# Table scatters moved ahead of the squares in the router's steps of an attention and mixture-of-experts kernel

## The chip, the cores and the metric

One core of a Trainium2 chip runs the whole program. The core has a matrix engine (TensorE, PE in the rows, with its weight loads as PEld), a vector engine (VectorE, DVE), an activation engine (ScalarE, ACT), a general engine (GpSimd, POOL) and an engine whose queue only issues DMAs here (SyncE, SP). Each works through its own queue in order and waits there for semaphores. The metric is the device time of one execution in microseconds (us), the median of the runs.

## What is computed

Block-causal attention over 8 batches, 8 heads, 576 places and a head size of 64, whose output rows are then routed, each to one of 8 experts:

```python
scores = np.where(block_i >= block_j, scale * q @ k.T, -1e9)     # blocks of 64
attn = softmax(scores);  x = (attn @ v) rearranged to (4608, 512)
xn = x / (norm(x) + 1e-6);  en = emb / (norm(emb) + 1e-6)
logits = xn @ en.T / tau
expert_idx = argmax(logits);  gate_w = softmax(logits)[expert_idx]
for e in range(8):
    h = relu(x[expert_idx == e] @ w1[e])
    out[expert_idx == e] = gate_w * (h @ w2[e])
```

## The kernel before

The attention takes the first 460 us or so, the experts the rest. The attention runs over 32 pairs of heads, four pairs for a batch. An iteration of its loop works on several pairs at once, each in another stage, and the order of the stages' steps is written out by hand: a string of letters (`PLANS`), one for each of the four places in a batch and four more for the last batch, in which each letter runs one step of a generator. Since each engine's queue is in order, these strings set the order of the work on all engines.

The letters: `s`, scores of the pair: PE's two matmuls (lines 368 and 369) into one of two PSUM buffers (`pss`), ACT's exp out of it (378, 385), POOL's adds of the exps over the key tiles (359), which later give the softmax sums. `v`, values of the pair before: matmuls of the exps with v (400), then the matmuls with ones over POOL's sums (409, 410, 414) and copies out by DVE (416) and ACT (418). `m`, row maxes of the next pair: PE's matmuls (337) into one of two buffers (`psm`), DVE's reductions out of them (339), at the end a transpose whose cast on ACT (346) is written into the queries' operand by SP (348). `p`, preparation two pairs ahead: transposes (296), casts on ACT (308, 312, 317), subtractions on DVE (287), copies by SP (310, 320). `f`, the finish of the pair before: transposes and matmuls (436 to 441) and DVE's scaling (446 to 459). `l`, loads. `r`, one step of the router, if one is at work.

The router of a batch (`route`, line 483) is appended when the batch's last pair is finished, which is in the first iteration of the next batch, and then gives one step to every `r`. It sums the heads' logits, takes the arg max as a one-hot `ohb`, counts the tokens ahead of each by small matmuls, and then, for all batches but the last:

- five `squares` (line 478): the sums of squares of the batch's 512-wide rows, on ACT, one for each tile of 128 tokens;
- the square root of them, a power on POOL (554);
- `table_rows` (634 to 644): six small DVE operations that give each token its place in a table in DRAM;
- the gate: add (558), reciprocal (560), product with the logits (562) on DVE, exp on ACT (564), sum, add and reciprocal on DVE (566 to 570), the last into the batch's rows `xrow`;
- `store` (473, 474): two DMAs on SP's queue that write the batch's rows with their gates, 1040 KB, to DRAM;
- five scatters (576): indirect DMAs that POOL issues, each writing 128 token numbers to the table at the places that `table_rows` gave. They don't read the squares, the gate or the rows.

Each of these operations ends its step, but the store is one step. Counted by the letters, in a usual batch the squares come at the end of the second iteration and the start of the third, power and table rows at places 11 to 23 of the third, the gate from place 39 of the third to place 3 of the fourth (in which values' sums, lines 409 to 414, stand at place 33), the store at place 5 and the scatters at places 6 to 12. After the scatters the router is done and the remaining letters `r` are empty. In the last-but-one batch, whose plans differ, a further generator (`early_rows`, 601 to 607) reads a part of the table back and gathers two tiles of rows.

Of the kernel before, what the change touches and what calls it, by code (L numbers as in the profile page):

```python
# [34 lines left out]
def kernel(  # L35
# [12 lines left out]
    nc = tc.nc  # L48
    B, H, S, D = q.shape
    E, DM, DF = w1.shape  # L50
    NT = B * S
    P = 128
    NP = H // 2
    NJ = (S - 64) // P + 1
# [16 lines left out]
    RE = (NT + P - 1) // P  # L71
# [3 lines left out]
    table = dram.tile([E * RE * P, 1], F32, name="table")  # L75
# [19 lines left out]
    def iota(name, shape, pattern, base=0, cm=0, dt=F32):  # L95
        t = const.tile(shape, dt, name=name)
        nc.gpsimd.iota(t, pattern=pattern, base=base, channel_multiplier=cm, allow_small_or_imprecise_dtypes=True)
        return t
# [3 lines left out]
    tokf = iota("tokf", [P, B, NJ], [[S, B], [P, NJ]], 1 - 64, 1)  # L102
# [377 lines left out]
    def bc(ap, *shape):  # L480
        return ap.to_broadcast(shape)

    def route(b, xrow, lgh, ssp):

        lg = sm.tile([P, NJ, E], F32, name="lg")
# [2 lines left out]
        ohb = sm.tile([P, NJ, E], BF16, name="ohb")  # L488
# [29 lines left out]
        if b < B - 1:  # L518
            t2 = above(rk, ebase)
# [11 lines left out]
        if b == B - 2:  # L531
# [11 lines left out]
            nc.vector.tensor_copy(accb, acc)  # L543
            yield

        ss = sm.tile([P, NJ], F32, name="ss")
        gs = sm.tile([P, NJ], F32, name="gs")
        if b < B - 1:
# [4 lines left out]
            nc.vector.tensor_reduce(ss, ssp, axis=AX.X, op=ALU.add)  # L553
        nc.gpsimd.tensor_tensor(ss, ss, half, op=ALU.pow)
        yield
        if b < B - 1:
            rowj = yield from table_rows(t2, ohb)
        nc.vector.tensor_scalar(ss, ss, 1.0e-6, None, op0=ALU.add)
        yield
        nc.vector.reciprocal(ss, ss)  # L560
        yield
        nc.vector.tensor_tensor(lg, lg, bc(ss.unsqueeze(2), P, NJ, E), op=ALU.mult)
        yield
        nc.scalar.activation(lg, lg, AF.Exp)
        yield
        nc.vector.tensor_reduce(gs, lg, axis=AX.X, op=ALU.add)
        yield
        nc.vector.tensor_scalar(gs, gs, 1.0e-9, None, op0=ALU.add)
# [3 lines left out]
        store(b, xrow, 0 if b < B - 1 else (NP - 1) * P, RW)  # L572
        yield
        if b < B - 1:
            for j in range(NJ):
                w = nc.gpsimd.indirect_dma_start(
                    out=table, out_offset=bass.IndirectOffsetOnAxis(ap=rowj[:, j:j + 1], axis=0),
                    in_=tokf[:, b, j:j + 1], in_offset=None, bounds_check=E * RE * P - 1, oob_is_err=False)
                for o in writes:
                    tc.declare_no_dep(w.ins, o.ins, reason="each place is written once")  # L580
                writes.append(w)
                yield
            if b == B - 2:
                slow.append(early_rows())

    writes, ends = [], []
# [25 lines left out]
    def above(rk, base):  # L612
        t = sm.tile([P, NJ, E], F32, name="t2")
        nc.vector.tensor_tensor(t, rk, base, op=ALU.add)
        return t
# [13 lines left out]
    def table_rows(t, ohb):  # L629

        row = sm.tile([P, NJ], F32, name="row")
        rowt = sm.tile([P, NJ], I32, name="rowt")
        rowj = sm.tile([P, NJ], I32, name="rowj")
        nc.vector.tensor_tensor(t, t, ohb, op=ALU.mult)
        yield
        nc.vector.tensor_reduce(rowj, t, axis=AX.X, op=ALU.max)
        yield
        nc.vector.tensor_scalar(rowt, rowj, P - 1, None, op0=ALU.bitwise_and)
        yield
        nc.vector.tensor_scalar(row, rowt, float(E * RE) - 1.0 / P, None, op0=ALU.mult)  # L640
        yield
        nc.vector.scalar_tensor_tensor(row, rowj, 1.0 / P, row, op0=ALU.mult, op1=ALU.add)
        yield
        nc.vector.tensor_tensor(rowj, row, drop, op=ALU.add)
        yield
        return rowj
# [460 lines left out]
    a, b = ea  # L1107
# [138 lines left out]
```

## Time and profile before

| | us |
|---|---|
| median of 3 runs | 943.08 (940.4 to 945.08) |
| profiled execution | 946.42 |
| its span, first to last instruction | 944.7 |
| PE busy | 903.0 (96%) |
| DVE, ACT, POOL busy | 536.0, 455.8, 335.5 |
| mean granted clock of PE | 0.976 |

The profiled execution has 1.7 us outside its span. Busy times count instructions at work; the granted clock is the share of full speed that the chip gave PE in a stretch. A timeline row gives an instruction's start, its duration, its engine and line, output and input tiles, and in brackets how long the engine had been idle and what released it.

### The profile page before, as it was taken

The numbers are of one execution on the slowest core, as the hardware profiler recorded it, in microseconds if no ns is written. First come the engines' busy times: TensorE is split into PE (matmuls) and PEld (weight loads), VectorE is DVE, ScalarE is ACT, GpSimd is POOL, SyncE is SP. The second block draws the span as 40 slices with busy tenths as digits, with TensorE's granted clock in tenths as the row PEclk, the third lists the DMA queues.
The fourth block names the chain that finished last, engine by engine and source line by source line (L and its number), as shares of the span: only waits on it lengthen the run. The fifth ranks groups of instructions, "written<-read, shape, count | busy, mean of one in ns | idle before, by whom it ended". The sixth has DMA issues, their size and how long they took to land. (4 is left out here: it accounts for less than half of the span.)

```text
span 944.7 us, 19846 instructions
## 1 busy us (share of the span) xinstructions
PE 903.0 (96%) x5429; PEld 706.8 (75%) x5429; DVE 536.0 (57%) x1291; ACT 455.8 (48%) x923; POOL 335.5 (36%) x436
## 2 busy tenths in 40 slices
PE   5999999898999989898999999999999999999996
PEld 4677677677766767665678888888888888888885
DVE  8678778686877858676676634664342222442221
ACT  4566658475565847566655424553432222432220
POOL 6444645556464555546631111111011111111111
PEclk8899989999999999899999999999999999999999
DMA  8958757676886758593737444654242111111101
GB/s 151 179 115 176 177 114 154 150 150 141 166 188 114 156 141 166 132 196 121 244 119 253 135 136 135 216 177 171 78 167 67 46 47 47 47 43 47 46 30 44
DMA packets 155248, 122.47 MB, mean 130 GB/s; under 512 B 122234, under 2 KB 123530, under 8 KB 155101
## 3 DMA queue, kind: packets, MB, share of 16 engines
q1 hardware_dynamic: 147372, 100.14, 44.0%
q0 software_dynamic: 7728, 20.70, 6.8%
q8 instruction: 52, 0.85, 0.4%
q14 instruction: 96, 0.78, 0.3%
HBM read 72.98 MB, written 19.71 MB: 98 GB/s over the span
## 5 line engine op out<-in xcount | busy, mean ns | idle before, releaser
L378 ACT ACTIVATE pT<-pss 128x448 f32<-128x448 f32 (+1 forms) x254 | 112.5, 452 | 111.9 <-PE pss L369 80.4
L339 DVE TENSOR_REDUCE nmx<-psm 128x1 f32<-128x320 f32 x315 | 135.1, 453 | 49.3 <-PE psm L337 38.7
L981 POOL DMA_INDIRECT out_dram<-y,outi x36 | 36.1, 1002 | 356.8 <-DVE y L980 336.6
L368 PE MATMUL pss<-qb,ka 128*128 128x448 f32 (+1 forms) x382 | 128.1, 346 | 17.9 <-ACT pT L378 17.0
L359 POOL TENSOR_TENSOR pS<-pT 128x448 f32<-128x448 f32 x64 | 73.1, 1142 | 155.3 <-ACT pT L378 155.0
L359 POOL TENSOR_TENSOR pS<-pS,pT 128x320 f32<-128x320 f32 (+2 forms) x192 | 114.2, 595 | 29.2 <-ACT pT L378 8.1
L941 PE MATMUL py<-ring_h,hh 128*128 (+1 forms) x288 | 116.4, 404 | 0.4 <-ACT hh L974 0.4
L941 PE MATMUL py<-ring_h,hl 128*128 (+1 forms) x288 | 113.6, 395 | 2.1 <-DVE hl L975 2.1
L941 PE MATMUL py<-ring_l,hh 128*128 (+1 forms) x288 | 112.7, 391 | 0.0
L369 PE MATMUL pss<-qx,kx 70*128 70x448 f32 (+1 forms) x382 | 110.4, 313 | 2.3 <-DMA qx<-nmT 2.3
L400 PE MATMUL psb<-pT,vo 128*64 128x64 f32 (+5 forms) x768 | 111.3, 405 | 1.2 <-DVE lgh L459 1.2
L941 PE MATMUL ph<-ring_h,xh 128*128 x280 | 112.2, 401 | 0.0
L941 PE MATMUL ph<-ring_h,xl 128*128 x280 | 109.7, 392 | 0.0
L941 PE MATMUL ph<-ring_l,xh 128*128 x280 | 109.3, 390 | 0.0
L933 DVE TENSOR_TENSOR xl<-px,xh 128x512 fp32r<-128x512 f32 x35 | 24.2, 690 | 145.4 <-ACTq L908 119.0
L368 PEld LDWEIGHTS pss<-qb,ka 128*128 128x128 f32 x382 | 74.6, 195 | 39.3 <-ACT pT L378 21.2
L974 ACT CAST hh<-px 128x512 fp32r<-128x512 f32 x72 | 38.7, 589 | 134.8 <-PE px L972 134.8
L959 ACT ACTIVATE h<-ph 128x512 f32<-128x512 f32 x70 | 41.8, 597 | 126.1 <-ACTq L908 58.5
L337 PE MATMUL psm<-kd,qd 128*128 128x320 f32 x315 | 91.7, 354 | 3.0 <-ACT kd L317 1.7
L761 DVE TENSOR_TENSOR ring_l<-raw,ring_h 128x1024 f32 (+1 forms) x64 | 77.3, 1248 | 25.3 <-ACT ring_h L757 25.1
L337 PEld LDWEIGHTS psm<-kd,qd 128*128 128x128 f32 x315 | 56.3, 196 | 40.4 <-ACT pT L385 14.6
L980 DVE TENSOR_SCALAR y<-py,xg 128x512 f32<-128x512 f32 x36 | 27.0, 750 | 98.9 <-PE py L941 93.4
(246 smaller groups left out, 1665.3 us busy)
## 6 DMA issues: line engine op xcount, KB each, us to landing
raw<-in_moe_w_dram SPq DMA_DIRECT2D x64, 512.0 KB
ka<-kd SPq DMA_DIRECT2D x128, 144.0 KB
qn<-in_q_dram SPq DMA_DIRECT2D x64, 144.0 KB
kn<-in_k_dram SPq DMA_DIRECT2D x64, 144.0 KB
qx<-qb SPq DMA_DIRECT2D x32, 288.0 KB
vo<-in_v_dram SPq DMA_DIRECT2D x64, 128.0 KB
xbuf<-xrow SPq DMA_DIRECT2D x7, 1040.0 KB
qx<-nmT SPq DMA_DIRECT2D x64, 2.2 KB
```

The costliest lines, as they stand in the source:

```text
L337: nc.tensor.matmul(mx[:, 0:max(e - a, 256)], qd[d][:, j, :, :], kd[d][:, a:a + max(e - a, 256)], start=True, stop=True)
L339: nc.vector.tensor_reduce(m[:, j + u:j + u + 1], mx[:, 0:e - a], axis=AX.X, op=ALU.max, negate=True)
L359: nc.gpsimd.tensor_tensor(o, pT[0:r, P:S] if t == 1 else o, pT[0:r, off[t]:off[t] + w], op=ALU.add)
L368: nc.tensor.matmul(o, ka[i][:, hh, ts], qb[i][:, hh, c0:c1], start=True, stop=False)
L369: nc.tensor.matmul(o, kx[i][0:KX, hh, ts], qx[i][0:KX, hh, c0:c1], start=False, stop=True)
L378: nc.scalar.activation(pT[:, o:o + c1 - c0], st[:, 0:c1 - c0], AF.Exp, scale=scale)
L400: nc.tensor.matmul(ob[hh * D:(hh + 1) * D, c0:c1], a[0:r, t, hh, :], pTs[hh][0][0:r, o:o + c1 - c0], start=(t == 0), stop=(c0 == 448 or t ...
L761: return eng.tensor_tensor(piece(ring_l, to, c, half), raw[i][:, c * CW:(c + 1) * CW], piece(ring_h, to, c, half).bitcast(F32), op=ALU.sub ...
L941: m = nc.tensor.matmul(out, a[:, c, :], w, start=(c == 0 and w is wh and a is sh), stop=(c == nk - 1 and a is sl_))
L959: nc.scalar.activation(h[:, f:f + 512], ph, AF.Relu)
L974: nc.scalar.copy(hh[:, f:f + 4, :], ptv)
L981: nc.gpsimd.indirect_dma_start(out=out, out_offset=bass.IndirectOffsetOnAxis(ap=to, axis=0), in_=y, in_offset=None, bounds_check=NT - 1, o ...
```

## The change

In `route`, for all batches but the last, `table_rows` and the five scatters stand ahead of the squares; the power follows the squares as before; then come seven empty steps, and the gate, with two empty steps ahead of its exp and five behind it. The store is the last step. No operation is added or taken away, and the plans are as before; the router takes 53 letters where it took 39.

```diff
+    def pause(n):
+        for _ in range(n):
+            yield
+
     def route(b, xrow, lgh, ssp):
...
+        if b < B - 1:
+            rowj = yield from table_rows(t2, ohb)
+            for j in range(NJ):
+                w = nc.gpsimd.indirect_dma_start(
+                    out=table, out_offset=bass.IndirectOffsetOnAxis(ap=rowj[:, j:j + 1], axis=0),
+                    in_=tokf[:, b, j:j + 1], in_offset=None, bounds_check=E * RE * P - 1, oob_is_err=False)
+                for o in writes:
+                    tc.declare_no_dep(w.ins, o.ins, reason="each place is written once")
+                writes.append(w)
+                yield
+
         ss = sm.tile([P, NJ], F32, name="ss")
         gs = sm.tile([P, NJ], F32, name="gs")
...
         nc.gpsimd.tensor_tensor(ss, ss, half, op=ALU.pow)
         yield
+
         if b < B - 1:
-            rowj = yield from table_rows(t2, ohb)
+            yield from pause(7)
         nc.vector.tensor_scalar(ss, ss, 1.0e-6, None, op0=ALU.add)
...
+        if b < B - 1:
+            yield from pause(2)
         nc.scalar.activation(lg, lg, AF.Exp)
         yield
+        if b < B - 1:
+            yield from pause(5)
         nc.vector.tensor_reduce(gs, lg, axis=AX.X, op=ALU.add)
...
         store(b, xrow, 0 if b < B - 1 else (NP - 1) * P, RW)
         yield
         if b < B - 1:
-            for j in range(NJ):
-                w = nc.gpsimd.indirect_dma_start(
...
-                yield
             if b == B - 2:
                 slow.append(early_rows())
```

By the letters, in a usual batch the table rows now come at the end of the second iteration and up to place 11 of the third, the scatters at places 13 to 21 of the third (values' sums stand at place 26), the squares at 23, 39, 40, 42 and 55, the power at 56; in the fourth iteration the gate's three first steps at places 12 to 16, its exp at 19, the rest at 34 to 37 and the store at 38, behind values' sums at 33. In the last-but-one batch, the squares come from the end of the second iteration on, the store at place 66 of the third, and the gathers in the fourth.

## Rows read from the trace of the kernel before

The stretch from 93.4 to 123.3 us holds the third and fourth iterations of batch 1, in which the router of batch 0 runs; the other batches repeat it every 55 us.

**Rows 1.** the page, section 1: busy us, share of the span, instructions.

```profile
PE 903.0 (96%) x5429; PEld 706.8 (75%) x5429; DVE 536.0 (57%) x1291; ACT 455.8 (48%) x923; POOL 335.5 (36%) x436
```

**Rows 2.** windows (stretch: length, each engine's busy us, granted clock, DMA share, GB/s).

```profile
55.00:67.70 12.70, 12.70 (x98) 9.22 (x98) 9.53 (x26) 7.70 (x17) 6.38 (x10) 1.00 0.42 90
105.50:123.30 17.80, 14.97 (x97) 11.12 (x97) 10.57 (x33) 8.18 (x18) 11.40 (x15) 0.86 0.45 124
...
sum 103.40, PE 87.66 PEld 64.74 DVE 63.46 ACT 48.47 POOL 67.67; mean PE 14.61 PEld 10.79 DVE 10.58 ACT 8.08 POOL 11.28
```

**Rows 3.** waits of PE, 50 to 480 us: total us, times, longest.

```profile
PE pss L368 <- ACT pT L378: 17.0, 7, 2.8
```

**Rows 4.** timeline, batch 0 (start us, us, engine, line; idle before and its releaser).

```profile
110.56 1.12 POOL L576 DMA_INDIRECT table<-tokf,rowj  x1 [0.58 <-DVE gs L566]
...
113.93 0.46 PE L410 MATMUL psb<-pS,ones 128*32 128x320 f32 x1
114.60 0.42 PE L368 MATMUL pss<-qb,ka 128*128 128x320 f32 x1
115.84 0.97 POOL L576 DMA_INDIRECT table<-tokf,rowj  x1 [0.30 <-issue]
116.82 1.15 POOL L359 TENSOR_TENSOR pS<-pT 128x448 f32<-128x448 f32 x1
118.12 0.44 ACT L378 ACTIVATE pT<-pss 128x320 f32<-128x320 f32 x1 [3.91 <-remote]
118.61 0.61 PE L368 MATMUL pss<-qb,ka 128*128 128x288 f32 x1 [2.83 <-ACT pT L378]
```

**Rows 5.** windows, the first 3.5 us behind that gap.

```profile
118.00:121.50 3.50, 2.89 (x12) 2.60 (x13) 3.02 (x7) 3.00 (x6) 1.76 (x3) 0.54 0.01 2
```

**Rows 6.** timeline of PE and window, last-but-one batch.

```profile
439.40 0.40 PE L368 MATMUL pss<-qb,ka 128*128 128x288 f32 x1 [1.24 <-ACT pT L378]
438.00:441.00 3.00, 1.60 (x10) 1.19 (x10) 1.47 (x3) 1.56 (x4) 2.65 (x4) 1.00 0.95 355
```

**Rows 7.** timeline of ACT, third iteration of batch 1 (squares of batch 0).

```profile
95.26 0.64 ACT L478 ACTIVATE xs<-xrow 128x512 f32<-128x512 f32 x1
...
102.37 0.44 ACT L378 ACTIVATE pT<-pss 128x320 f32<-128x320 f32 x1 [0.47 <-PE pss L369]
...
104.90 0.41 ACT L378 ACTIVATE pT<-pss 128x288 f32<-128x288 f32 x1
...
105.80 0.96 ACT L378 ACTIVATE pT<-pss 128x288 f32<-128x288 f32 x2
```

**Rows 8.** timeline of PE, the same iteration.

```profile
106.01 0.66 PE L296 MATMUL pst<-ident,kn 96*128 96x96 f32 x6
106.46 0.39 PE L368 MATMUL pss<-qb,ka 128*128 128x320 f32 x1
```

**Rows 9.** timeline of POOL, the same iteration and the next.

```profile
99.09 1.21 POOL L554 TENSOR_TENSOR ss<-ss,half 128x5 f32<-128x5 f32 x1 [1.69 <-ACT xs L478]
...
106.83 1.14 POOL L359 TENSOR_TENSOR pS<-pT 128x448 f32<-128x448 f32 x1 [0.70 <-ACT pT L378]
108.05 1.93 POOL L359 TENSOR_TENSOR pS<-pS,pT 128x320 f32<-128x320 f32 x3
```

**Rows 10.** timelines of DVE and PE, the same stretch.

```profile
99.44 0.62 DVE L339 TENSOR_REDUCE nmx<-psm 128x1 f32<-128x448 f32 x1
...
110.17 0.49 DVE L339 TENSOR_REDUCE nmx<-psm 128x1 f32<-128x320 f32 x1
110.97 0.85 PE L337 MATMUL psm<-kd,qd 128*128 128x512 f32 x2
```

**Rows 11.** windows of 2 us, third and fourth iteration.

```profile
102.00:104.00 2.00, 2.00 (x16) 1.81 (x16) 1.86 (x6) 1.60 (x4) 1.92 (x2) 1.00 1.32 212
...
114.00:116.00 2.00, 1.78 (x20) 1.36 (x20) 0.57 (x2) 0.21 (x1) 1.39 (x3) 1.00 1.01 363
```

**Rows 12.** timeline of PE, the sums' matmuls of the third iteration.

```profile
101.10 0.46 PE L410 MATMUL psb<-pS,ones 128*32 128x320 f32 x1
```

More of the change, by code (lines that the diff above doesn't have):

```diff
@@ L574, in route @@
         if b < B - 1:
-            for j in range(NJ):
-                w = nc.gpsimd.indirect_dma_start(
[L577 to L581, printed above, removed]
-                yield
             if b == B - 2:
```

## The prediction, made before the changed kernel was run

> **What bounds the kernel now.** I read the page's busy times first: TensorE (PE) works in 96% of the span [rows 1], so a change of a few microseconds must either remove idle or slowed PE time or add some. Next the span was cut into its 32 pair iterations, from one cast of the maxes (line 346) to the next, and each was read as a window. An iteration that is the fourth of its batch and has no router to run takes 12.70 us, with PE busy throughout and the granted clock 1.00. The first that has the end of a router in it takes 17.80 us: 2.83 us idle, and the same 97 matmuls take 14.97 us at a mean granted clock of 0.86. Together the six such iterations (one for each of batches 0 to 5) last 103.40 us with 87.66 us of PE work [rows 2]. The second and third iterations, in which the rest of the router stands, show no idle PE. The list of PE's waits gives the same place: line 368 waits for the exp of line 378, seven times, 17.0 us in all [rows 3].
>
> The timeline of batch 0 shows what happens there. POOL runs five scatters from 110.56 to 116.81 (a new one every 1.3 us). PE works on meanwhile: the sums of line 410 start at 113.93, the scores of line 368 at 114.60. But the exp that reads those scores starts only at 118.12 after 3.91 us of idle, for which the view has no releaser ("remote"). That is 1.31 us after the last scatter's end; PE itself has then been idle for 2.83 us, since the scores' two buffers are full [rows 4]. No operand of that exp comes from POOL. So the results of PE are seen late when the sums' matmuls run beside the scatters and the store; the trace doesn't show which of those two is to blame. After the gap the granted clock is 0.54 [rows 5], the lower of the two levels (1.2 GHz) for most of that window. In the last-but-one batch the same wait is 1.24 us, and the granted clock stays at 1.00 in the 3 us around it [rows 6].
>
> **What the change takes away.** The store and the scatters no longer run together: the scatters stand in the third iteration, before the sums of squares, and the store of batch b stands behind the sums' matmuls of the fourth, alone. If that ends the stall, the gain is 103.40 - 87.66 = 15.74 us of idle, 87.66 - 6 x 12.70 = 11.46 us of slow clock, and 1.24 us in the last-but-one batch: 28.4 us.
>
> **What it adds: nothing in number, but new neighbours.** The same instructions run; the empty steps cost only places. The squares are five ACT operations with a read of 0.2 us each, one every 0.76 us, from 95.26 to 99.09 [rows 7, 9]. Before, they stand in a slot in which ACT has nothing else. After, the first comes just ahead of the exp at 102.37, the next three behind the exp at 104.90, in a stretch where ACT has little room (it is busy 1.60 of the 2 us from 102 [rows 11]). The first square delays what follows by about 0.4 us: it takes 0.76, and finds the 0.47 of idle time at 102.37 [rows 7], less its own start. With PE's part of that delay the exp of 104.90 ends at 105.84 instead of 105.31; three squares put 2.27 us behind it, to 108.11; the cast of the maxes (0.3 us) and the next exp (105.80 before, 0.4 us) end at 108.85. PE's scores of 106.46 need the buffer that this exp frees, so they start at 108.85 instead of 106.46: **2.4 us** later. PE's own work ahead of them, the six transposes at 106.01, ends at 107.1 with its share of the delay, so about 1.8 us of it is one gap [rows 8]. Bounds: 0 (if what waits were all absorbed) to 3.8 us (all five squares); I take 2.4, as the order on ACT is fixed by the steps.
>
> POOL: the places are ready after DVE's reduction of 99.44, at about 100.3 [rows 10]. Five scatters at batch 0's spacing take 6.25 us, so 100.4 to 106.65. The adds of a head take 3.15 us (106.83 to 109.98), those of two heads 6.3, to 113.0; the power (1.21 us) that stood at 99.09, before them, now follows at 114.3 [rows 9]. The next step of the chain is a DVE operation after seven empty steps, just behind the reduction that stood at 110.17, or 2.4 us later, about 112.8. It **blocks DVE's queue** until 114.3. Behind it stand reductions of maxes, for which PE's line 337 (110.97 before) waits, with two buffers [rows 10]: PE could issue the second of those two (0.4 us later) at 113.7 and gets its buffer at 114.3 + 0.5 = 114.9: **1.2 us**. Bounds: 0, if seven steps are enough, to 2.0. Together 3.6 us for a batch, 21.6 us for six.
>
> A rule speaks against the new position too. The scatter at 110.56 took 1.12 us and that at 115.84, while DVE was idle, 0.97 [rows 4]. The Trainium skill ("DMA: Bandwidth & Descriptors", section "SWDGE vs HWDGE vs iDMA") says that the rings that GpSimd writes its descriptors to are SBUF state out of which DVE's fast two-port mode locks it; by it the five scatters would take up to 5 x 0.15 = 0.75 us more beside a busy DVE, an estimate from those two rows, and the sum would be some 4.5 us higher. No row shows it at that size for all five, and my sum doesn't have it.
>
> The clock: a gap of 2.83 us was followed by 0.54, that of 1.24 us by full speed [rows 4 to 6]. The new gaps of 1.8 and 1.2 us lie between, so their cost is 0 to 11.46 / 6 = 1.9 us for a batch; I take half, 5.7 us in all. The last-but-one batch has its router's steps elsewhere and ends with a store and two gathers later than before: 0 to 3.6 us (one batch's waits), taken as 1.2.
>
> **The sum**, against the profiled execution's 946.42 us: -28.4 + 21.6 + 5.7 + 1.2 = +0.1. The median of the runs is 3.3 us below that execution, so 943 us, **no change**; with the clock's and the last batch's bounds, 936 to 951.
>
> **What costs nothing.** The store's two DMAs stay in SP's queue in the same iteration; they now stand behind the copies of the next pair's queries (line 310), which gain by that, and ahead of the loads two thirds further down the plan. At the 363 GB/s that it reached [rows 11] a store of 1040 KB takes 2.9 us, so the loads find it gone; if not, they come a part of that later, and PE needs them only two pairs on. In the last-but-one batch the loads of weights stand behind it, which is in that batch's bound. On POOL's queue the adds of two heads now wait behind the scatters, as costed; in the fourth iteration they stand behind none. The steps of the table's rows (six DVE operations under 0.2 us) move ahead by half an iteration into gaps of DVE; if they delay a reduction, it is by less than one of them, 0.2 us a batch.
>
> **Rival one, faster.** The delays on ACT and DVE are partly absorbed and leave gaps too short for the clock. With the DVE wait gone (POOL's power in time) and only the gap of 1.8 us left: -28.4 + 6 x 1.8 = -17.6, **925 us** (915 if nothing is left). For it: DVE and ACT have a half of their time idle elsewhere, and 1.24 us passed without a slower clock. Against it: in this iteration PE has no idle time to give, and ACT is full.
>
> **Rival two, slower: the late results move with the scatters.** In the third iteration the sums' matmuls (line 410) stand at 101.10 [rows 12], inside the new 100.4 to 106.65. If scatters beside these matmuls are the cause, with a DMA load like the store's, PE's results are again seen only 1.31 us after the last scatter, at 107.96. The loads are there: the DMA share is 1.32 at 102 to 104, against 1.01 with the store [rows 11]. The exp of 102.37 [rows 7] would then start 5.6 us late; with 1.9 us of slow clock 7.5 a batch, 6 x 7.5 - 28.4 = +16.6, **960 us**, and with the squares' 2.4 on top 974. It decides from a hold of over 4.7 us a batch, clock included. For it: every one of the six batches has both conditions. Against it: the loads are no writes to DRAM, and in the last-but-one batch, where adds stand between scatters, the hold was shorter.
>
> **Rival three: the change doesn't do what it says.** If the store alone makes PE's results late, the stall stays where it is, behind the sums, and the new waits come on top: +21.6 with little change of the clock, 943 + 22 = **965 us**. Against it: the release came right after POOL's first add behind the scatters (116.82 and 1.15 us, so 117.97 [rows 4]), and nothing of the store ends there.
>
> **Chances.** Forecast 0.42 (of which 0.28 within 0.5%, 0.07 on each side); rival one 0.27; rival two 0.24; rival three 0.07. A measurement of this kernel can tell about 0.5%, 4.7 us, from no change. So faster 0.27 + 0.07 = 0.34, same 0.28, slower 0.24 + 0.07 + 0.07 = 0.38. The range leaves out the lower part of rival one and the upper part of rival two, 0.1 each: 922 to 966 us.
>
> **What would show it.** Right: in the fourth iterations no exp of line 378 waits for "remote"; in the third ones the list of PE's waits has line 368 waiting for an exp of line 378 by 1.5 to 2 us in each batch, with squares just before that exp on ACT's timeline; DVE's first operation on the gate waits for POOL's power until some 6 us after the cast of the maxes (346) with which the fourth iteration begins. Wrong: exps in the third iterations that wait for "remote" during the scatters (rival two); a fourth iteration that still has 2.5 us of idle PE (rival three); third iterations of under 13 us (rival one).

## The result: 1.3% slower, and where the time went

The changed kernel took 956.85 us (median of 5 runs, 952.89 to 957.85) against 941.71 us for the kernel before in the same session: a ratio of 1.0131 (95% interval 1.0111 to 1.0151). Ratios here are formed from the single runs without slow ones (there is one, of 968.83 us, in after_again below), so they differ a little from the quotient of two medians, which is 1.0161 here. The forecast was no change, 943 us, with 922 to 966 as its range. So the time lay inside the range and the sign was wrong: slower, and clear of the 0.5% that can be told from nothing.

The profiled executions flatter the change: that of before was 4.7 us above the median of its runs, that of after, 952.89 us, is 4.0 us below its own. The page of after, section 1:

```profile
span 951.1 us, 19846 instructions
PE 906.4 (95%) x5429; PEld 703.3 (74%) x5429; DVE 535.9 (56%) x1291; ACT 453.7 (48%) x923; POOL 335.3 (35%) x436
```

Four windows of it, each one iteration from one cast of the maxes to the next: the third of batch 1, its fourth, the first of batch 2, and the third of the last batch, in which the last-but-one batch's router runs. The columns are those of [rows 2].

```profile
94.90:108.60 13.70, 13.21 (x103) 9.81 (x101) 11.09 (x33) 8.58 (x21) 8.38 (x10) 1.00 0.86 167
108.60:123.10 14.50, 12.48 (x90) 8.40 (x89) 9.59 (x29) 9.85 (x27) 9.60 (x13) 1.00 0.24 63
123.10:137.90 14.80, 13.87 (x107) 10.07 (x106) 10.40 (x30) 8.63 (x20) 5.84 (x8) 1.00 1.02 234
428.20:445.60 17.40, 15.41 (x92) 11.41 (x91) 10.26 (x27) 10.84 (x33) 11.98 (x14) 0.80 0.16 39
```

The iteration that answers to the last row, in the kernel before:

```profile
429.00:443.30 14.30, 12.48 (x91) 8.49 (x90) 10.36 (x34) 7.16 (x27) 11.17 (x14) 1.00 0.45 127
```

PE's waits from 50 to 480 us, to hold against [rows 3]:

```profile
PE psm L337 <- DVE nmx L339: 8.4, 14, 1.4
PE pe L940 <- DMA ex<-xbuf,ei: 4.3, 2, 2.4
PE pss L368 <- ACT pT L378: 4.3, 7, 1.7
PE pss L369 <- DMA qx<-nmT: 4.2, 5, 1.0
PE pss L368 <- issue: 2.9, 6, 0.5
```

The 17.0 us of line 368 have become 4.3. In their place stand waits that before had little or nothing of: for a reduction of DVE (8.4 us), for the gathered rows at the end (4.3), for the maxes' row (4.2, a DMA) and what is left of line 368 (4.3, and 2.9 with no releaser but "issue"). Iteration by iteration, over batches 0 to 5: the third ones went from about 12.05 to between 13.6 and 13.9 us, the fourth ones from 16.7 to 17.8 down to between 14.1 and 14.5 (one 16.6, at a lower clock), most first ones from about 14.0 to 14.8. Together the iterations of these six batches got 2.1 us shorter. The net loss in this pair of traces is at the end: the last two iterations before 445.6 us are 2.9 us longer, and what follows is 4.1 us longer.

The timelines of POOL, ACT, PE, DVE, PE and SP, with batch 0's router in after, show the new waits of a usual batch:

```profile
102.34 1.11 POOL L553 DMA_INDIRECT table<-tokf,rowj  x1 [3.49 <-DVE rowj L656]
...
110.74 0.99 POOL L553 DMA_INDIRECT table<-tokf,rowj  x1 [0.39 <-ACT pT L385]
...
114.89 1.21 POOL L569 TENSOR_TENSOR ss<-ss,half 128x5 f32<-128x5 f32 x1
...
107.22 0.63 ACT L478 ACTIVATE xs<-xrow 128x512 f32<-128x512 f32 x1
...
107.98 0.63 ACT L478 ACTIVATE xs<-xrow 128x512 f32<-128x512 f32 x1
...
108.61 0.24 ACT L346 CAST nmT<-psm 9x128 fp32r<-9x128 f32 x1
108.75 0.82 ACT L378 ACTIVATE pT<-pss 128x288 f32<-128x288 f32 x2
...
109.20 0.42 PE L368 MATMUL pss<-qb,ka 128*128 128x320 f32 x1 [0.49 <-ACT pT L378]
...
116.13 0.17 DVE L574 TENSOR_SCALAR ss<-ss 128x5 f32<-128x5 f32 x1 [2.52 <-POOL ss L569]
...
117.42 0.44 PE L337 MATMUL psm<-kd,qd 128*128 128x384 f32 x1 [1.37 <-DVE nmx L339]
...
127.63 0.40 PE L369 MATMUL pss<-qx,kx 70*128 70x288 f32 x1 [0.93 <-DMA qx<-nmT]
...
121.39 0.59 SPq L474 DMA_DIRECT2D xbuf<-xrow  x1
...
123.33 2.73 SPq L348 DMA_DIRECT2D qx<-nmT  x2
```

The scatters run beside the adds from 102.34 to 111.73. Two squares (107.22, 107.98) stand ahead of the cast of the maxes and of the exp at 108.75, for which PE waits 0.49 us at 109.20. The power ends at 116.10, and DVE's first operation on the gate has waited 2.52 us for it; PE then waits 1.37 us for a reduction behind it. And the store (121.39) stands in the DMA queues ahead of the maxes' row, which is issued at 123.33 and lands late: PE waits 0.93 us at 127.63. (In best, a kernel below whose store comes early, no first iteration of these batches has this wait.)

At the end, first ACT and PE in the iteration of the last-but-one batch's router, with a window behind the gap, then POOL and PE behind it:

```profile
435.49 0.63 ACT L478 ACTIVATE xs<-xrow 128x512 f32<-128x512 f32 x1
...
436.12 0.69 ACT L378 ACTIVATE pT<-pss 128x288 f32<-128x288 f32 x2
...
436.56 0.47 PE L368 MATMUL pss<-qb,ka 128*128 128x448 f32 x1 [1.67 <-ACT pT L378]
...
440.00:443.00 3.00, 3.00 (x14) 2.68 (x14) 2.26 (x5) 0.90 (x2) 2.77 (x5) 0.50 0.00 0
...
458.17 1.12 POOL L619 DMA_INDIRECT ex<-xbuf,ei  x1 [0.17 <-issue]
...
462.18 1.11 PE L940 MATMUL pe<-ident,ex 128*128 128x128 f32 x4 [2.43 <-DMA ex<-xbuf,ei]
```

In that iteration ACT does nothing but squares from 430.29 to 436.2: five of the finish, 128 columns wide, and then the router's five. PE waits 1.67 us for the exp behind them and then works at a granted clock of 0.50. That slow clock is what makes the iteration longer: 17.40 us at 0.80 with 1.99 us of idle PE, against 14.30 at 1.00 with 1.82. after_again and after_c3 below have the same wait, 1.66 us; in squares_pow_old, with squares and power early, the iteration takes 13.5 us at full clock.

The two gathers of the last-but-one batch's router start at 458.17; PE wants their rows at about 459.7 and waits 2.43 us for the first and 1.88 us for the second. No such wait is in the list of the kernel before.

### The profile page after: what moved, and what is told of

Read it like the earlier page. It is cut to its first block, busy times and chain, and to the rows that moved or that the text cites. A ratio compares the mean times of both kernels' runs of the same rounds, so it can differ in the third digit from the quotient of the medians.

```text
span 951.1 us, 19846 instructions
## 1 busy us (share of the span) xinstructions
PE 906.4 (95%) x5429; PEld 703.3 (74%) x5429; DVE 535.9 (56%) x1291; ACT 453.7 (48%) x923; POOL 335.3 (35%) x436
## 5 line engine op out<-in xcount | busy, mean ns | idle before, releaser
L359 POOL TENSOR_TENSOR pS<-pS,pT 128x320 f32<-128x320 f32 (+2 forms) x192 | 113.9, 593 | 28.6 <-ACT pT L378 13.6
L337 PE MATMUL psm<-kd,qd 128*128 128x320 f32 x315 | 94.8, 361 | 10.4 <-DVE nmx L339 8.4
```

The costliest lines, as they stand in the source:

```text
L337: nc.tensor.matmul(mx[:, 0:max(e - a, 256)], qd[d][:, j, :, :], kd[d][:, a:a + max(e - a, 256)], start=True, stop=True)
L359: nc.gpsimd.tensor_tensor(o, pT[0:r, P:S] if t == 1 else o, pT[0:r, off[t]:off[t] + w], op=ALU.add)
```

## Experiments

All compare with the kernel before in the same session. One finding stands ahead of the rest, since it decides how the others are read: **the kernel before itself came in two kinds of session**. In four sessions it took 942 to 944 us, as above, in three others 918.6 to 919 us; nothing lay between, and the same numbered chip was seen in both kinds. I call the first kind "held" and the second "free"; before_c3 shows what the difference is. The expectations, written ahead of the runs, still speak of a chip with or without the hold.

### Is it the end, the squares or the power? (held session, before 944.5 us)

after_again is the changed kernel once more.

> The changed kernel once more, for a second trace of it. Its first profiled execution took 952.89 us with a mean granted clock of 0.989, the other four 954.9 to 957.9 with 0.973 to 0.979. If the difference is the clock, a trace at 0.975 has its extra 3 to 5 us in iterations whose granted clock is below 1, at the same waits as in the first trace (third iterations of a batch 13.7 to 13.9 us, fourth 14.1 to 14.5 and up to 16.6 where the clock fell). If it is other waits, iterations at a clock of 1.00 are longer. Median 955 to 957 us.

959.52 us (median; 953.29 to 967.31), above the 955 to 957 expected; ratio 1.0176 (1.0121 to 1.0231). Windows of three fourth iterations:

```profile
108.10:122.50 14.40, 12.41 (x90) 8.31 (x89) 9.27 (x26) 9.80 (x26) 9.58 (x13) 1.00 0.24 61
163.80:180.80 17.00, 15.65 (x95) 11.33 (x93) 9.84 (x29) 9.91 (x27) 9.31 (x13) 0.81 0.37 108
387.00:405.00 18.00, 16.14 (x89) 11.43 (x89) 9.41 (x28) 9.88 (x26) 9.38 (x13) 0.75 0.33 101
```

The second and third have 1.35 and 1.86 us of idle PE, as the first has 2.0, but granted clocks of 0.81 and 0.75. In this trace three fourth iterations lost 2 to 3.7 us that way, in the first trace one. So the spread of the changed kernel's runs is the clock behind the new gaps, which falls in some batches and not in others at nearly the same gap; over its runs the time goes from 952.89 us at a mean granted clock of 0.989 to 967.31 at 0.965.

last_old leaves the last-but-one batch in the old order:

```diff
-        if b < B - 1:
+        if b < B - 2:
             rowj = yield from table_rows(t2, ohb)
             for j in range(NJ):
                 w = nc.gpsimd.indirect_dma_start(
...
+        if b == B - 2:
+            rowj = yield from table_rows(t2, ohb)
...
-        if b < B - 1:
-            if b == B - 2:
-                slow.append(early_rows())
+        if b == B - 2:
+            for j in range(NJ):
+                w = nc.gpsimd.indirect_dma_start(
...
+            slow.append(early_rows())
```

> The changed kernel with the old order of the router for the last-but-one batch alone (batches 0 to 5 as changed). Theory one (the loss is the end: the table is read back later, so the two gathers come later and PE waits 4.3 us for them, and one iteration is 3 us longer): 7 us less than the changed kernel, about 949.5 us, with no wait of PE for the gathered tiles. Theory two (the loss is spread over the batches): 1 us less at most, about 956 us.

947.73 us, ratio 1.0042 (1.0021 to 1.0063): 12 us less than after_again. The wait for the gathered rows is gone, and the iteration of the last-but-one batch is back at its old length:

```profile
431.10:445.30 14.20, 12.45 (x90) 8.46 (x89) 10.21 (x34) 7.12 (x27) 11.12 (x14) 1.00 0.45 128
```

By the two traces 3.0 us of the 12 lie in the last two iterations and 5.4 behind them; 3 us lie in batches 0 to 5, where the clock fell in three fourth iterations of one trace and in two of the other. Theory one holds, and the end costs 7 to 8 us.

squares_old puts the squares back to where they were, all else as changed, with empty steps in their place; squares_pow_old puts the power ahead of the scatters as well (the line with `pow`, which squares_old doesn't have). Both do so for the last-but-one batch too:

```diff
...
         if b < B - 1:
-            rowj = yield from table_rows(t2, ohb)
+            rows = table_rows(t2, ohb)
+            for j in range(NJ):
+                squares(xrow[:, j, 0:DM], ss[:, j:j + 1])
+                next(rows)
+                yield
+            nc.gpsimd.tensor_tensor(ss, ss, half, op=ALU.pow)
+            rowj = yield from rows
...
```

> The changed kernel with the five squares back at their old places (in the same steps as the first five operations of the table rows; five empty steps where they stood). Scatters, power, gate and store stay as changed. If the squares in ACT's full stretch are what lengthens the third iterations from 12.05 to 13.85 us, these return to about 12.1 and the time falls by 6 x 1.7 = 10 us to about 947 us. If it is PE's results that are seen late beside the scatters, the third iterations stay at 13.5 or more and the time at 955 us.

> As squares_old, with the power on POOL ahead of the scatters too. If DVE waits for POOL's power in the fourth iterations (1.04 to 1.37 us of idle PE at line 337), this wait goes and the fourth iterations fall from 14.15 to about 12.8 us: 6 x 1.3 = 8 us less than squares_old, about 939 us. If the fourth iterations are long for another reason, as squares_old, 947 us.

squares_old took 971.55 us, ratio 1.0293 (1.0258 to 1.0328): slower than the changed kernel, where 947 or 955 was expected. The third and fourth iterations of batch 1, and PE in the second of them:

```profile
93.00:105.70 12.70, 12.21 (x95) 8.98 (x94) 10.29 (x30) 10.89 (x28) 7.36 (x9) 1.00 0.97 181
105.70:123.60 17.90, 15.57 (x97) 11.40 (x96) 10.35 (x33) 8.13 (x18) 10.60 (x14) 0.84 0.36 102
...
115.55 0.44 PE L337 MATMUL psm<-kd,qd 128*128 128x384 f32 x1 [2.17 <-DVE nmx L339]
```

The third one fell from 13.7 to 12.7 us. That is not what the squares cost PE: a cast on ACT ends the iteration, the squares had delayed that cast, and PE had gone on meanwhile (103 matmuls in the third iteration of after and 90 in the fourth, 95 and 97 here). What they cost PE shows at the next wait. The power comes no earlier than before, since it waits for POOL's adds and not for the squares: in both kernels it ends 22.2 to 22.5 us after the third iteration's start. PE comes to it 0.4 to 0.8 us earlier, so that much the squares had cost; the gaps there are now 1.46 to 2.17 us where they were 1.04 to 1.37, and in all six batches the clock falls (0.84 in this row). The 0.5 us of idle PE in the third iteration is another wait. A delay taken away in one stage was given back, and more, in the next. With the power early the same fourth iteration is:

```profile
107.30:120.60 13.30, 13.12 (x98) 9.36 (x97) 11.32 (x33) 7.93 (x19) 9.45 (x13) 1.00 0.29 69
```

939.25 us, ratio 0.9953 (0.9932 to 0.9973). Fourth iterations of 13.2 to 13.6 us at full clock: the power on DVE's path was the fourth iterations' loss, as the forecast's mechanism had it.

### Is the gain there? (free sessions, before 918.6 us)

The next four were made to see what holds PE's results. In scat_at_sums the store's step comes 14 steps behind the scatters, in store_at_sums the scatters come 18 steps behind the store, in both_behind store and scatters come 16 steps later. The edit of store_at_sums; the others are alike:

```diff
         store(b, xrow, 0 if b < B - 1 else (NP - 1) * P, RW)
         yield
         if b < B - 1:
+            if b < B - 2:
+                yield from pause(18)
             for j in range(NJ):
                 w = nc.gpsimd.indirect_dma_start(
...
```

best is squares_pow_old with the last-but-one batch old and one empty step in all.

> The kernel before with the store of batches 0 to 5 moved 14 steps behind the scatters, so that the scatters alone stand beside the values' sums in the fourth iteration and the store comes behind both. If PE's results are held by scatters beside the sums, whatever the DMA queues carry, fourth iterations stay at about 17 us and the time at 944 to 950 us. If it takes scatters and a saturated DMA (the store) together, fourth iterations fall to 12.7 to 13.3 us; the store then stands where the changed kernel has it, ahead of the maxes' row, which costs about 0.8 us in each first iteration: 6 x (-4.6 + 0.8) = -23, about 921 us.

> The kernel before with the scatters of batches 0 to 5 moved 18 steps behind the store, so that the store alone stands beside the values' sums. If the store alone holds PE's results, fourth iterations stay at 17 us and the time at 944 us. If scatters are needed, they fall to 12.7 to 13.3 us: 6 x -4.6 = -28, about 917 us, unless the scatters' 6.3 us of POOL at the end of the iteration delay the adds of the next one, which would show as idle PE there.

> The kernel before with store and scatters of batches 0 to 5 together, as they are, but 16 steps later, behind the values' sums. If the sums' matmuls are part of the cause, the long wait for a 'remote' releaser goes and fourth iterations fall to about 13 to 14 us, the time to about 925 us. If a saturated DMA beside scatters is enough, PE's results are held as long there, at another matmul: 944 us or more.

> squares_pow_old with two more edits: the last-but-one batch in the old order, and no empty steps but one ahead of the exp, so that the gate and the store of batches 0 to 5 come as early in the fourth iteration as before, scatters in the third. By the accounts of the runs so far: squares_pow_old 939 us, less 4.7 us of PE waiting for the gathered tiles, less 6 x 0.8 us of waiting for the maxes' row behind the store: about 930 us. If the store beside the sums holds PE's results alone, fourth iterations become 17 us and the time 955 us.

scat_at_sums 917.52 us (ratio 0.9982, 0.9954 to 1.001), store_at_sums 926.22 (1.0071, 1.0045 to 1.0097), both_behind 926.4 (1.0069, 1.0038 to 1.01), best 928.87 (1.0106, 1.0068 to 1.0143). The session was a free one, and nothing in any of the traces was held, so none tells the theories apart. scat_at_sums also failed as a design: empty steps don't delay a DMA when no other DMA is queued between, so its store was issued as early as before (at 112.10 us, behind the first scatter and right behind the operation that gives its data, which ends at 112.04). What the others do show is the price of scatters late in the iteration: the adds of the next pair wait behind them, first iterations take 14.4 us instead of 13.7, and one iteration of the last batch has 1.9 us of idle PE for a sum of POOL.

best came out at the 930 us that were expected from held sessions, but loses to before here. Its fourth iterations have 1.3 to 1.5 us of idle PE. The longest gap, 0.5 to 0.7 us of that, in rows of POOL, DVE and PE:

```profile
105.43 1.16 POOL L359 TENSOR_TENSOR pS<-pT 128x448 f32<-128x448 f32 x1
...
105.15 1.48 DVE L580 TENSOR_SCALAR ss<-ss 128x5 f32<-128x5 f32 x1
...
107.69 0.71 PE L296 MATMUL pst<-ident,kn 96*128 96x96 f32 x6 [0.69 <-DVE qb L287]
```

The gate's first operation, an add on 128x5 numbers, takes 0.17 us in after, but 1.48 us here, and ends when POOL's add ends (105.43 and 1.16 us). DVE's subtraction behind it is what PE's transposes wait for.

Then the kernel before and the changed one in one free session, with late_store, which moves the gate's sum and so, by its data, the store behind the values' sums, and best again:

```diff
+        if b < B - 2:
+            yield from pause(3)
+            for j in range(NJ):
+                w = nc.gpsimd.indirect_dma_start(
...
+            yield from pause(10)
         nc.vector.tensor_reduce(gs, lg, axis=AX.X, op=ALU.add)
```

> The kernel before, for its trace on this chip. The chip of the first comparison runs it in 942 to 944 us with PE's results held beside the scatters (fourth iterations 17 us), the chip of the last four runs in 918.6 us. If the difference is that hold, a trace at 942 us has it in all of batches 0 to 5, and one at 918 us has fourth iterations of 12.7 to 12.8 us and no exp that waits for 'remote'; nothing between.

> The changed kernel. On a chip with the hold: 953 to 962 us, ratio about 1.015. On a chip without it nothing is gained, and the new waits remain (1.0 us for the squares in each third iteration, 1.3 us and some slow clock for POOL's power in each fourth, 0.8 us in each first, 7 us or more at the end): 918.6 + 6 x 3.1 + 7 = 944 us and up, ratio about 1.03.

> The kernel before with the gate's sum, its reciprocal and so the store of batches 0 to 5 behind the values' sums, the scatters where they were. On a chip with the hold: if it takes scatters and the store's traffic together, fourth iterations fall from 17 to 12.7 to 13.3 us and first ones stay at 14 to 14.9: about 922 us; if scatters beside the sums' matmuls are enough, fourth iterations stay at 16.7 us or more: 944 us or more. On a chip without the hold: 918 to 924 us, the store being the only cost.

> The kernel called best again. On the chip of the last runs it took 928.9 us (before: 918.6), with 1.35 us of idle PE in each fourth iteration. On a chip with the hold: its fourth iterations as there, 14.6 us, third ones 12.1 us plus 0.6 for results held beside the scatters: 918.6 + 10 + 6 x 0.6 = 932 us, under the 943 us of before.

before_c3 took 923.67 us (one run; the other runs of before beside it have a median of 918.59). Its fourth iteration as a window, to hold against [rows 2]:

```profile
107.90:120.70 12.80, 12.80 (x98) 9.23 (x98) 10.55 (x31) 8.07 (x18) 9.89 (x13) 1.00 0.63 172
```

and from the timeline of the same stretch a scatter and the exp beside it, to hold against [rows 4]:

```profile
116.95 0.97 POOL L576 DMA_INDIRECT table<-tokf,rowj  x1 [0.30 <-issue]
...
117.58 0.44 ACT L378 ACTIVATE pT<-pss 128x320 f32<-128x320 f32 x1 [0.98 <-PE pss L369]
```

12.80 us instead of 17.80, with the same store, scatters and sums side by side. The exp that waited 3.91 us for "remote" starts 0.98 us after the one before, released by PE. So the stall that the change was forecast to remove is no property of the schedule alone: in this free session it doesn't exist.

after_c3 took 968.69 us, ratio **1.0496** (1.0455 to 1.0537). With nothing to gain, all that is left are the costs. Windows of a third iteration, a fourth, and the 3.5 us behind its gap:

```profile
95.40:108.50 13.10, 13.10 (x103) 9.81 (x101) 11.15 (x34) 8.58 (x21) 7.78 (x9) 1.00 0.88 175
108.50:127.30 18.80, 16.33 (x90) 11.52 (x89) 9.49 (x28) 9.91 (x27) 10.20 (x14) 0.75 0.33 97
118.00:121.50 3.50, 3.50 (x21) 2.15 (x22) 2.28 (x6) 0.11 (x1) 1.13 (x1) 0.50 0.00 0
```

DVE and PE at that gap:

```profile
116.64 0.17 DVE L574 TENSOR_SCALAR ss<-ss 128x5 f32<-128x5 f32 x1 [3.14 <-POOL ss L569]
...
117.93 1.23 PE L337 MATMUL psm<-kd,qd 128*128 128x384 f32 x2 [1.98 <-DVE nmx L339]
```

The third iteration is 1.05 us longer than 12.05, with no idle PE and 103 matmuls in it; the fourth is 5.8 to 6.0 us longer than 12.8, with 90. The two together have 2.47 us of idle PE in this batch, 0.49 behind the squares (at line 368) and 1.98 behind the power, and then PE's matmuls run at a granted clock of 0.50, the lower level. This happens in all six batches; with 0.5 us in the first iterations that is 7.4 x 6 = 44 us, and the end adds 6.4 by the two traces. That is the 50 us between the medians. late_store took 918.0 us (0.9987, 0.9958 to 1.0017): where nothing is held this later store costs nothing. best_c3 took 930.5 us, as before.

### How much is the power? (free session, before 919.1 us)

more_pause has 14 empty steps ahead of the gate and none in its middle:

```diff
-            yield from pause(7)
+            yield from pause(14)
...
-        if b < B - 1:
-            yield from pause(2)
...
-        if b < B - 1:
-            yield from pause(5)
```

> The changed kernel with its empty steps moved: fourteen ahead of the gate's first operation instead of seven, none ahead of its exp and none behind. If DVE's wait for POOL's power is what leaves 1.1 to 2.0 us of idle PE in the fourth iterations, and that gap is what lowers the clock, both go: fourth iterations of 18.6 us (chip without held results) or 14.1 to 18 us (chip with them) become about 13 us, that is 6 x 5.9 = 35 us less than the changed kernel on the first (969 to about 934 us), 8 to 15 us less on the second (957 to about 946 us). If the clock falls for another reason, fourth iterations stay over 16 us where they were.

> late_store again, which on the chip without held results took 918.0 us (before: 918.6). On a chip with them: if it takes scatters and the store's traffic together, fourth iterations are 12.7 to 13.3 us and the time about 922 us against 943 us; if scatters beside the sums' matmuls are enough, fourth iterations stay at 16.7 us or more and the time at 943 us. On a chip without them, 918 us again, which tells nothing new.

951.49 us, ratio 1.0347 (1.0298 to 1.0396), not the 934 expected; late_store_c4 919.24 us (1.0001). DVE's wait for the power is gone, and fourth iterations fell from 18.6 to 15.5 us. But:

```profile
114.59 1.14 POOL L359 TENSOR_TENSOR pS<-pT 128x448 f32<-128x448 f32 x1 [0.25 <-ACT pT L378]
...
114.79 0.96 DVE L574 TENSOR_SCALAR ss<-ss 128x5 f32<-128x5 f32 x1
...
117.74 0.85 PE L337 MATMUL psm<-kd,qd 128*128 128x256 f32 x2 [1.22 <-DVE nmx L339]
```

The gate's add again takes 0.96 us, beside POOL's add of 114.59, and with the other steps close together the reductions come late once more: PE waits 1.22 us, and the clock still falls (0.89 over the iteration). So the empty steps have a use once the power is there in time: they keep DVE's small operations off POOL's adds.

### What holds PE's results (held sessions, before 943 us)

repaired is squares_pow_old with the last-but-one batch in the old order.

> squares_pow_old (squares in their old places, power ahead of the scatters, all else as changed) with the last-but-one batch in the old order. If squares, power and last batch are the whole loss of the change, what is left of it is a move of scatters, gate and store that costs nothing where PE's results are not held: 918 to 922 us on such a chip (the changed kernel: 969), with third iterations of 12.1 and fourth of 12.8 to 13.3 us. On a chip with the hold: 939.3 less 5 to 9 us for the last batch, 930 to 935 us, against 943. If another part of the change costs, it stays over 930 us on the first kind of chip.

> late_store a third time, for a chip with held results. There: fourth iterations of 12.7 to 13.3 us and about 922 us against 943 if it takes scatters and the store's traffic together; 16.7 us or more and 943 us if scatters beside the sums' matmuls are enough. On a chip without the hold 918 to 919 us again.

> repaired once more. Where the kernel before runs in 943 us (PE's results held beside scatters) it took 935.7 us. Where the kernel before runs in 919 us: 918 to 922 us if squares, power and last-but-one batch are the whole loss of the changed kernel there (969 us); over 930 us if another part of the change costs too.

> store_at_sums once more: the store beside the values' sums, the scatters behind them, at the end of the fourth iteration and into the first. Where results are not held it took 926 us (before: 918.6), by adds that wait behind the scatters. Where they are held: if the sums' matmuls are what must stand beside the scatters, no exp waits for a 'remote' releaser in the fourth iterations, these take 12.8 us and first ones 14.4, and the time is about 926 us against 943. If any matmul beside scatters is held, the wait moves to the end of the fourth or into the first iterations with 2.5 us of idle PE, and the time stays at 943 us or more.

Both sessions were held ones. repaired took 935.73 us (0.9932, 0.9905 to 0.9958) and 933.94 us (0.9911, 0.9879 to 0.9944): a gain, a third of what the stall is worth. Its traces still have 0.5 us of idle PE in each third iteration and 0.5 to 1.0 us in each first one, behind the store. What it takes in a free session was not measured, so it isn't shown that squares, power and end are the whole loss there.

late_store_c5 took 944.07 us (1.0012, 0.9994 to 1.003). The timelines of PE, POOL, SP and ACT in a fourth iteration:

```profile
115.38 0.46 PE L410 MATMUL psb<-pS,ones 128*32 128x320 f32 x1
...
117.43 0.97 POOL L573 DMA_INDIRECT table<-tokf,rowj  x1 [0.30 <-issue]
...
117.16 0.60 SPq L474 DMA_DIRECT2D xbuf<-xrow  x1
...
119.40 0.44 ACT L378 ACTIVATE pT<-pss 128x320 f32<-128x320 f32 x1 [3.74 <-remote]
```

and a window of it:

```profile
114.00:116.00 2.00, 2.00 (x24) 1.25 (x20) 1.32 (x4) 1.61 (x3) 1.54 (x2) 1.00 0.02 0
```

In the window from 114 to 116, in which the sums' matmuls begin, the DMA queues move next to nothing (share 0.02), and the store's second part is issued at 117.16, when the exp was already late (in the free session it came 1 us after the one before, which here would be 116.6). Yet the exp starts only at 119.40, after 3.74 us and 1.0 us after the last scatter, much as in [rows 4]. So **neither the store nor full DMA queues are needed** for results to be held. store_at_sums_c6, with the scatters behind the sums, took 924.87 us, ratio **0.9808** (0.9784 to 0.9832), the fastest kernel of a held session. Its fourth and next first iteration:

```profile
105.40:118.20 12.80, 12.80 (x98) 9.24 (x97) 10.58 (x31) 8.07 (x19) 6.67 (x10) 1.00 0.61 171
118.20:132.70 14.50, 14.38 (x107) 9.96 (x106) 10.80 (x30) 8.68 (x20) 10.60 (x14) 1.00 0.87 164
```

12.80 us at full clock, in a held session, with the store beside the sums. Its scatters run beside matmuls of lines 296, 337, 344, 368, 369, 400 and 441, and no exp is held. So of the kinds of matmul that run beside the scatters in before only the sums' (lines 409 to 414) are missing here, and these are by elimination what the hold needs. The pair alone doesn't set its length: in the third iterations of after and repaired the sums also run beside scatters, and PE waits 0.5 us. What in a session makes it hold stays open. Nor was it tried which of the sums' matmuls is the one; those of lines 410 and 414 read sums that POOL has just written.

## Why the prediction was wrong, step by step

**What bounds the kernel** was read rightly: where a trace has idle or slow PE, its iterations are longer by at least as much.

**The gain** (28.4 us) was sized rightly for held sessions: no exp of a fourth iteration waits for "remote" in after, and store_at_sums_c6, which takes the stall away at little cost elsewhere, gained 18 us with 0.7 us lost in each first iteration and an iteration that grew by 3 us at the end. Rival three (the store alone) fell: late_store_c5 has the hold, in batch 0 before its store is issued. But the gain is there in held sessions only.

**The squares**, 2.4 us a batch, cost 0.4 to 0.8 (squares_old against after; 0.49 of idle PE in after_c3). The mechanism was as described, PE waiting for an exp behind squares, but only two of them stand ahead of the maxes' cast and not four. I had counted the letters two places too early: the router is appended only when the finish's generator is drained at the end of its iteration, not at its last `f`, so all places given by letters in the sections above are two letters `r` too early. The timelines show the true ones.

**The power on DVE's path**, 1.2 us, was right in place and order, on the operation named, and its size, 1.04 to 1.37 us in the first trace, came out in part by luck: the letters were two places off, and the scatters began at 102.34 and not at 100.4, with adds between them. In a free session, where PE comes to it earlier, it is 1.8 to 2.0.

**The clock** was the term with too small a bound. I took 0.95 us a batch, at most 1.9 from the old stall. Where the clock fell, a fourth iteration lost 2 to 4 us: in one batch of the first trace, three of the second, six of six in the one trace of a free session. That a gap of 1.24 us had left it alone in [rows 6] was no bound: more_pause lost clock behind 1.22 us, and after_again behind 1.01.

**The last-but-one batch** is the step that failed by most: 1.2 us taken, 0 to 3.6 as its bounds, 7 us by the first pair of traces, 8 by those of after_again and last_old. I bounded it by the waits of a usual batch, and not by what hangs on its end: the gathers, which follow the router's last step, start 9 us later than before, and PE has a fixed time at which it wants the rows. That is some 4 us. The trace of before had the numbers (gathers from 449.4, PE's first use at 458.4). The other 3 are the slow clock behind the 1.67 us at the squares, which in this batch follow five others on ACT; the squares' term was worked out for a usual batch alone.

**The store**: I let it cost nothing, behind the copies of queries and ahead of loads. It stands just ahead of the maxes' row, 2.2 KB that PE needs in the next iteration: 0.5 to 1.0 us in each first iteration of the first trace where the clock had not already made PE late. (Its two DMAs write 130 and 1040 KB, not 1040 together.)

**Rival two** came true in a small size. In held sessions PE has about 0.5 us of idle time in each third iteration while the scatters run (line 368, "issue", six times), and these take 13.6 to 13.9 us against 13.1 in free ones: 0.65 us a batch, not 5.6. The scatters stand apart there, with adds between them, and no exp waits for the last one; whether that is because they stand apart was not tried.

The rule of the Trainium skill ("DMA: Bandwidth & Descriptors", section "SWDGE vs HWDGE vs iDMA") speaks of DVE's two-port mode and could have made the scatters longer beside a busy DVE. No run shows it at that size: the first took 1.11 us and the later ones 0.98 to 1.02 in after too.

Taken together in the first pair of traces: 27.2 us gained in the fourth iterations; 19.6 lost in third and fourth ones, 3.0 in the first ones and 7.1 at the end, so 2.5 us lost, and with one batch of slower clock (2.5 us) and 1.5 us at the start, ahead of any router, nearly the 6.4 us by which the spans differ. Of the 19.6 us the waits named are 12.1 (power 6.9, hold 2.9, squares 2.3); the rest is shorter waits and busy time of PE, about 1 us a batch, that no view puts down to a cause. The medians differ by 15 us, since the profiled execution of before lies 4.7 us above its median and that of after 4.0 below; after_again's trace, of 959.52 us, has two more batches of slower clock, 6 us. That the time still fell inside the range is in part luck: the squares, counted at 14 us for six batches, cost 3 to 4, and that made up for the store and rival two's hold, 3 to 4 us each, which the sum had at nothing, and for some of the end.

## What to carry to other kernels

Cost a moved chain by its last consumer: what starts when the chain ends, and which engine waits for it at a fixed time, above all in the last round of a loop. Where an operation of one engine waits in the queue of another that feeds the matrix engine, move the producer (here the power ahead of the scatters) and not the consumer; and a delay removed ahead of such a wait is no gain until the wait is gone. Before a stall is planned away, look whether it is there in more than one session.

## What the runs showed of the hardware

- PE's results can be seen late while POOL issues indirect DMAs beside matmuls that read POOL's output: in twelve fourth iterations (before, late_store_c5) an exp came after 3.6 to 3.9 us of idle ACT, 1.0 to 1.3 us after the last of five scatters, with the DMA queues full of a store (share 1.01, batch 0 of before) or nearly empty (0.02, batch 0 of late_store_c5) when it began. The same program had none of it in other sessions, 943 against 919 us, and it was the session, not the numbered chip, that differed.
- A small DVE operation can last until POOL's operation beside it ends: the gate's add on 128x5 numbers took 0.17 us in after, 0.96 in more_pause, 1.48 in the row of best, and it ends with POOL's add (115.75 and 115.73; 106.63 and 106.59). The Trainium skill ("SBUF — State Buffer", section "🔬 SBUF: two separate sides") says that DVE, in a two-port mode or with two inputs in SBUF, and GpSimd share a pair of ports under an exclusive lock for a whole instruction. These rows agree, though none shows in which mode the add ran.
- The granted clock went to 0.50 behind gaps of 1.0 to 2.2 us of idle PE in some batches (1.01 in after_again, 2.17 in squares_old) and stayed at 1.00 behind gaps of 1.0 to 1.4 us in others (1.37 in after). The length of the gap alone doesn't tell.
- Empty steps delay no DMA by themselves: in scat_at_sums SyncE's queue issued the store 0.06 us after the operation that gave its data, at 112.10, though 14 empty steps and the scatters stood between.
